# One Trainium2 core: attention, routed experts and a dense layer, with queries in their own order, maxima masked by products, and residues split anew between VectorE and GpSimd

## The chip, the cores and the metric

The kernel runs on one core of a Trainium2 chip. Its time is the device time in microseconds from start to end of one execution; the kernel before took 931.68 us, the median of three runs.

## The reference

Three layers follow each other. Only the first, the attention, is touched by the change.

```python
# q, k, v: (4, 8, 576, 64), s: (4, 8, 576), all float32
scores = scale * np.matmul(q, k.transpose(0, 1, 3, 2))          # scale = 1 / 8
cum = np.cumsum(np.maximum(s, 0.0), axis=-1)
bias = -(cum[:, :, :, None] - cum[:, :, None, :])
scores = np.where(causal, -1e9, scores + np.minimum(bias, 0.0)) # causal: j > i
attn = np.exp(scores - np.max(scores, axis=-1, keepdims=True))
attn = attn / (np.sum(attn, axis=-1, keepdims=True) + 1e-09)
x = np.matmul(attn, v)                                          # -> (2304, 512)
# then: gate = softmax(x @ w_gate), the best of 8 experts for each row:
#   out = gate * (max(x @ w1[e], 0) @ w2[e])                    # 512 -> 1024 -> 512
# then: h = max(out @ w_in, 0); h * h @ w_out                   # 512 -> 2048 -> 512
```

## The kernel before

**Precision.** Each number that goes into a product of the attention is held as two float16 numbers, a high part and a low part (the number less its high part). So every q, k and v is first cast (the high part, lines 428 to 432) and then subtracted (the low part, lines 438 and 441), and the exponentials are split as well: H is the exponential in float16, P the same in float32, and L = P - H the residue.

**Tiling.** The 32 pairs of batch and head (n = 0 to 31) are worked in 8 units u of 4 heads. A unit has tiles kA, qA (both parts of k and q, head dimension on the partitions, made by DMA transposes at line 477 from hlk and hlq) and, three deep in turn, kB and qB (the high part once more, on 64 partitions, with rows for the cumulative bias and for the maxima below them). A head's 576 rows are four blocks of 128 and a tail of 64. In qB the queries stand in another order than in q: `load` fetches them four rows a partition, so the copies into qB (line 501, one a head, and 506, the tails) put them back in order with a strided read; `second_k` (line 559) copies the keys into kB in two pieces.

**Steps of a head.** `maxima` works on pairs of heads: products of the high parts (line 586) into the PSUM tiles mxb and mxt, then on VectorE a maximum over each row's block (line 592: it adds a mask from SBUF while it reads, writes a junk tile, and is followed by an instruction that reads the accumulator out; line 624 is the one maximum that needs no mask). Lines 645 and 646 make high and low parts of the maxima, TensorE transposes them (652), lines 654 or 655 copy them to ms, and a DMA (658) puts them as two rows into qB. Only then can `scores` multiply (lines 679 and 680, with a mask product at 682). `expo` makes P (732) and H (734) on ScalarE, both from the PSUM tile of the scores, and L (736) on GpSimd or VectorE. `pv` multiplies v with H and L (767), and the sums and the division follow (786 to 797). Every few heads the gate of the experts works on finished rows (line 892 and on).

**What sets the order.** `Steps` is a planner: it holds a cost per engine for each step, what the step needs, its buffers and its due time, and lays out one fixed list of instructions per engine. Where a step may go on several engines (`st.add` with several costs) the planner chooses. On the chip each engine works through its list in order, waiting where data are not ready. Gaps that the planner sees on TensorE it fills with products that nobody reads (lines 317 and 324).

After the attention, at about 272 us, the expert and dense loops begin; no line of them is changed.

Of the kernel before, what the change touches and what calls it, by code (L numbers as in the profile page):

```python
# [19 lines left out]
NEG = -1.0e30  # L20
# [154 lines left out]
class Attention:  # L175
# [5 lines left out]


# [7 lines left out]
    LDVE = 6  # L190

    def __init__(self, ctx, tc, keep, q, k, v, s, w_gate, x_dram, tab, base, base0, ident):
# [22 lines left out]
        tags(5, "P")  # L215
        tags(10, "H", "L")
        tags(3, "junk", "ms")
# [46 lines left out]
    def setup(self, moe_constants):  # L264
# [7 lines left out]
        self.mrow, self.mtail = tile("mrow", [128, 512], F32), tile("mtail", [128, 64], F32)  # L272
        self.mT, self.mTt = tile("mT", [128, 128], BF16), tile("mTt", [64, 64], BF16)
        self.tops, self.parts = tile("tops", [128, NP, 9], F32), tile("parts", [128, NP, 18], F16)
# [19 lines left out]
        def mrow():  # L294
            nc.gpsimd.memset(self.mrow, 0.0)
            for i in range(4):
                block(self.mrow[32 * i:32 * i + 32, 384:512], [[-1, 128]], i, 4)

        def mtail():
            nc.gpsimd.memset(self.mtail, 0.0)  # L300
            for i in range(2):
                block(self.mtail[64 * i:64 * i + 64, :], [[-1, 64]], 0, 1)

        def mT():
            nc.gpsimd.memset(self.mT, 0.0)
            block(self.mT.rearrange("j (c p) -> j c p", c=4), [[1, 4], [4, 32]], 0, -1)
# [5 lines left out]
        self.gps("mrow", 1670, mrow)  # L312
# [20 lines left out]
        self.gps("mtail", 700, mtail)  # L333
# [4 lines left out]
    def decay(self):  # L338
# [46 lines left out]
    def load(self, u, w):  # L385
        b, h0 = u // 2, 4 * (u % 2)
        use = [("ld" + w, u)]
        for h in range(0, 4, 2 if w == "q" else 1):
            if w == "q":

                f = lambda eng, h=h: eng.dma_start(
                    out=self.ld(w, u)[:, 4 * h:4 * h + 8, :].rearrange("p (o c) d -> p o (c d)", o=2),
                    in_=self.src[w][b, h0 + h:h0 + h + 2, 0:512, :].rearrange("o (p c) d -> p o (c d)", c=4))
            else:
                f = lambda eng, h=h: eng.dma_start(
                    out=self.ld(w, u)[:, 4 * h:4 * h + 4, :],
                    in_=self.src[w][b, h0 + h, 0:512, :].rearrange("(t p) d -> p t d", p=128))
            self.dma(("ld", w, u, h), f, 730, use=use)
# [13 lines left out]
    def split(self, u, w, eng=None):  # L412
# [31 lines left out]
        for p in pieces:  # L444
            n = 128 if p == "t" else 256 * p[1]
            if p == "t":
                need, use = [("tl", w, b, o) for o in range(2)], [("tl" + w, b), (out, u)]
            else:
                need = [("ld", w, u, h) for h in range(p[0], p[0] + p[1], 2 if w == "q" else 1)]
# [3 lines left out]
            if w != "v" and u < self.LOU:  # L453
                self.st.add(("lo", w, u, p), {"DVE": 1.04 * n + 65, "Pool": 2.1 * n + 90}, lambda e, p=p: lo(p, e),
                            need=[("hi", w, u, p)], use=use)
            else:
                self.dve(("lo", w, u, p), n, lambda p=p: lo(p), need=[("hi", w, u, p)], use=use)
        return pieces

    def turns(self, u):  # L460
# [8 lines left out]
        for i, (b0, nb, gs, what) in enumerate(groups):  # L469
# [11 lines left out]
            need = [("turn", "k", u, i)] + [("eights", "k", u, g) for g in gs if u < 3]  # L481
            if u > 2:
                need.append(("kb", u - 1, 0, "m"))
            for x in what:
                self.dve(("kb", u, i, x), 32 * (nb - nb // 9 if x == "m" and nb > 8 else nb // 9 if nb > 8 else nb),
                         lambda x=x, gs=gs: self.second_k(u, x, gs), need=need, use=[("kA", u), ("kB", u)])
                self.same([("kbx", u, x, g) for g in gs], ("kb", u, i, x))
        gs = (1,) if u == 0 else (0, 1)
        self.dma(("extra", u), lambda eng: self.extra(u, 2 * gs[0], eng), 40, need=["rows"] + (
# [5 lines left out]
        use = [("qA", u), ("qB", u)]  # L495
        for g in range(2):
            pre = [("eights", "q", u, g)] if u < 3 else [("qt", u - 1, 0)]
            for o in range(2):
                h = 2 * g + o
                cs = self.cols(h, 0, 512)  # L500
                self.dve(("qb", u, h), 132, lambda cs=cs: nc.vector.tensor_copy(
                    out=qB[:, cs].rearrange("r (i c p) -> r i c p", c=4, i=4), in_=self.order(A("q")[64:128, cs])),
                    need=pre + [("turned", "q", u, "m", g)], use=use)
        for gs in ((0, 1),) if u else ((0,), (1,)):
            g = slice(gs[0], gs[-1] + 1)
            self.dve(("qt", u, gs[0]), 128 * len(gs) / 4, lambda g=g: nc.vector.tensor_copy(
                out=qB.rearrange("r (g c) -> r g c", g=2)[:, g, 1024:1152],
                in_=A("q")[64:128].rearrange("r (g c) -> r g c", g=2)[:, g, 1024:1152]),
                need=[("turned", "q", u, "t", x) for x in gs] + ([("eights", "q", u, x) for x in gs] if u < 3 else
                                                                 [("qt", u - 1, 0)]), use=use)  # L510
            self.same([("qtail", u, x) for x in gs], ("qt", u, gs[0]))

    def first_turns(self, pieces):
# [3 lines left out]
        for w in "kq":  # L517
            dst = lambda w=w: self.tile(w + "A", 0, [128, 2304], F16)
            for x, b0, nb in ((0, 0, 4), (1, 4, 4), ("t", 8, 1)):
# [18 lines left out]
                if w == "k":  # L538
                    d = slice(512, 576) if x == "t" else slice(576 * x, 576 * x + 512)
                    def second(e, d=d, ps=ps, x=x):  # L540
                        out, src = self.kB[0][0:64, d], ps()[0:64]
                        if x == "t":
                            out = self.kB[0][0:64, 0:1152].rearrange("r (o t) -> r o t", o=2)[:, :, 512:]
                            src = src.rearrange("r (o t) -> r o t", o=2)
                        (nc.scalar.copy if e == "ACT" else nc.vector.tensor_copy)(out=out, in_=src)
# [7 lines left out]
    def second_k(self, u, x, gs):  # L553

        g = slice(gs[0], gs[-1] + 1)
        src = self.tile("kA", u)[0:64].rearrange("r (g c) -> r g c", g=2)[:, g]
        src = (src[:, :, 0:1024] if x == "m" else src[:, :, 1024:]).rearrange("r g (o t) -> r g o t", o=2)
        dst = self.kB[u % 3][0:64].rearrange("r (g o t) -> r g o t", g=2, o=2)[:, g]
        self.nc.vector.tensor_copy(out=dst[:, :, :, 0:512] if x == "m" else dst[:, :, :, 512:], in_=src)

    @staticmethod
    def order(a):
        return a.rearrange("r (c i p) -> r i c p", c=4, i=4)

# [7 lines left out]
    def maxima(self, n):  # L572
# [12 lines left out]
        def mm(out, h, i0, M, j0, N):  # L585
            nc.tensor.matmul(out=out, lhsT=qB[:, self.cols(h, i0, M)], rhs=kB[:, self.S * h + j0:self.S * h + j0 + N],  # L586
                             start=True, stop=True)

        def red(ps, in1, col, init=None):
            w = ps.shape[-1]  # L590
            junk = self.pools["junk"].tile([128, 512], BF16, tag="junk", name=f"junk{n}")
            nc.vector.tensor_tensor_reduce(out=junk[:, 0:w], in0=ps, in1=in1, scale=1.0,  # L592
                                           scalar=2 * NEG if init is None else init,
                                           op0=ALU.add, op1=ALU.max, accum_out=st[:, col:col + 1])
# [5 lines left out]
        def b1r(o, ps):  # L600
            red(ps[:, 0:128], self.mrow[:, 384:512], 4 * o)
            red(ps[:, 128:512], self.mrow[:, 128:512], 4 * o + 2)

# [16 lines left out]
        todo = [("b1", o, 512, lambda ps, o=o: b1(o, ps), 580, lambda ps, o=o: b1r(o, ps)) for o in range(2)]  # L620
        todo += [("b2", o, 512, lambda ps, o=o: mm(ps, h + o, 384, 128, 0, 512), 512,
                  lambda ps, o=o: red(ps, self.mrow, 4 * o + 3)) for o in range(2)]
        todo += [("b3", 0, 512, b3, 580, b3r),
                 ("t1", 0, 520, t1, 512, lambda ps: nc.vector.tensor_reduce(out=st[:, 8:9], in_=ps, axis=AX.X, op=ALU.max)),  # L624
                 ("t2", 0, 66, t2, 126, lambda ps: red(ps[:, 0:64], self.mtail, 8, init=st[:, 8:9]))]
        done = []
        for nm, o, cols, f, el, r in todo:
# [3 lines left out]
            need += [("cum", u, i, g) for i in os] + ([("z", u)] if u > 2 else [])  # L631
# [1108 lines left out]
```

## Time and profile before

| | |
|---|---|
| median of 3 runs | 931.68 us (931.45 to 933.04) |
| the profiled execution, its own time | 932.99 us |
| its span, first to last instruction | 931.5 us |
| mean granted TensorE clock | 0.967 |
| busy over the span: PE, DVE, ACT, POOL | 859.1, 691.9, 479.5, 330.1 us |

A busy share is a mean over stages that differ: the attention (to about 246 us), the handover with the gate's last part (to about 272 us), and the experts and the dense layer. PE, DVE, ACT, POOL and SP are TensorE, VectorE, ScalarE, GpSimd and SyncE.

### The profile page before, as it was taken

The numbers are of one execution on the slowest core, as the hardware profiler recorded it, in microseconds if no ns is written. First come the engines' busy times: TensorE is split into PE (matmuls) and PEld (weight loads), VectorE is DVE, ScalarE is ACT, GpSimd is POOL, SyncE is SP. The second block draws the span as 40 slices with busy tenths as digits, with TensorE's granted clock in tenths as the row PEclk, the third lists the DMA queues.
The fourth block names the chain that finished last, engine by engine and source line by source line (L and its number), as shares of the span: only waits on it lengthen the run. The fifth ranks groups of instructions, "written<-read, shape, count | busy, mean of one in ns | idle before, by whom it ended". The sixth has DMA issues, their size and how long they took to land.

```text
span 931.5 us, 17578 instructions
## 1 busy us (share of the span) xinstructions
PE 859.1 (92%) x6561; PEld 730.5 (78%) x6561; DVE 691.9 (74%) x1404; ACT 479.5 (51%) x1012; POOL 330.1 (35%) x367
## 2 busy tenths in 40 slices
PE   4887977879889999999999999999999999999995
PEld 2566755657689999998999777888888888888894
DVE  8999999998856888899889885554455445444673
ACT  3566766656624454455456444444444445444563
POOL 8858677664642364356333351010001000100100
PEclk9988999888979999999999999999999999999998
DMA  7875885880166766866665300010001000000100
GB/s 150 147 144 114 171 164 146 147 170 3 38 181 221 227 194 191 275 207 213 203 221 174 120 1 1 1 45 1 1 1 46 0 1 11 36 1 0 46 1 24
DMA packets 142780, 94.06 MB, mean 101 GB/s; under 512 B 98484, under 2 KB 127630, under 8 KB 142690
## 3 DMA queue, kind: packets, MB, share of 16 engines
q1 hardware_dynamic: 134385, 78.72, 32.7%
q0 software_dynamic: 4096, 10.19, 3.3%
q10 hardware_dynamic: 4209, 3.97, 1.4%
q8 instruction: 53, 0.87, 0.4%
q14 instruction: 37, 0.30, 0.1%
HBM read 70.16 MB, written 10.02 MB: 86 GB/s over the span
## 4 chain that ended last, share of the span: by engine, by line
PE 58%; issue 6%; DVE 5%; ACT 1%; POOL 0%; POOLq 0%; DVEq 0%; ACTq 0%
PE y_d L1556 7%; PE hd L1476 7%; PE hd L1474 7%; PE hd L1475 7%; PE y_d L1554 6%; PE y_d L1555 6%; PE y_e L1494 3%; PE y_e L1495 3%; PE y_e L1493 3%; PE he L1474 3%; PE he L1475 3%; PE he L1476 3%; DVE wae_6l L1404 1%; DVE wbe_6l L1404 1%; DVE wbe_7l L1404 1%
## 5 line engine op out<-in xcount | busy, mean ns | idle before, releaser
L1599 POOL DMA_INDIRECT out_dram<-o,ids x18 | 18.5, 1027 | 341.9 <-ACT o L1596 339.1
L1542 DVE TENSOR_TENSOR sqd<-hd,rld 128x512 f32<-128x512 f32 (+1 forms) x80 | 50.9, 637 | 112.8 <-ACT rld L1540 111.7
L736 POOL TENSOR_TENSOR L<-P,H 128x512 f16<-128x512 f32 x87 | 104.8, 1218 | 53.6 <-ACT H L734 25.4
L1540 ACT ACTIVATE rld<-hd 128x512 f32<-128x512 f32 (+1 forms) x80 | 44.5, 556 | 130.8 <-PE hd L1476 130.8
L1546 DVE TENSOR_TENSOR ald<-sqd,ahd 128x512 fp32r<-128x512 f32 (+1 forms) x80 | 51.1, 639 | 51.6 <-ACT ahd L1545 51.6
L1545 ACT CAST ahd<-sqd 128x512 fp32r<-128x512 f32 (+1 forms) x80 | 46.3, 579 | 74.2 <-DVE sqd L1542 74.2
L1456 POOL TENSOR_TENSOR lf<-lf,pw 128x512 f32<-128x512 f32 x32 | 50.1, 1566 | 73.4 <-DVE pw L1455 55.1
L732 ACT ACTIVATE P<-tt 128x512 f32<-128x512 f32 x96 | 58.3, 610 | 32.9 <-PE tt L682 14.5
L680 PE MATMUL tt<-qB,kB 128*128 128x128 f16 (+3 forms) x352 | 64.4, 236 | 0.0
L767 PEld LDWEIGHTS <-H 128*128 128x128 f16 x896 | 51.1, 101 | 14.4 <-issue 8.9
L734 ACT ACTIVATE H<-tt 128x512 f16<-128x512 f32 x96 | 58.3, 612 | 6.8 <-PE tt L680 3.8
L1483 ACT ACTIVATE hhe<-he 128x400 fp32r<-128x400 f32 (+7 forms) x64 | 27.9, 436 | 65.1 <-PE he L1476 60.5
L767 PE MATMUL pv<-v,H 128*128 128x65 f16 (+1 forms) x896 | 60.8, 200 | 0.6 <-ACT xb L797 0.3
L679 PE MATMUL tt<-qA,kA 128*128 128x128 f16 (+3 forms) x352 | 59.3, 235 | 1.1 <-ACT H L734 0.9
L592 DVE CUSTOM_DVE_ANT_0 junk<-mxb,mrow 128x128 bf16<-128x128 f32 (+3 forms) x128 | 55.1, 484 | 2.9 <-PE mxb L586 2.6
L767 PE MATMUL pv<-v,L 128*128 128x65 f16 x448 | 55.7, 197 | 1.3 <-DVE L L736 0.8
L1181 POOL DMA_INDIRECT xg<-x_dram,idt x20 | 21.2, 1060 | 85.5 <-PE xps L1191 69.5
L586 PE MATMUL mxb<-kB,qB 128*128 128x128 f16 (+3 forms) x128 | 32.0, 338 | 18.0 <-DVE tops L624 9.5
L767 PEld LDWEIGHTS <-L 128*128 128x128 f16 x448 | 44.1, 103 | 1.5 <-DVE L L736 0.9
L1484 DVE SCALAR_TENSOR_TENSOR hle<-he,hhe 128x400 fp32r<-128x400 f32 (+7 forms) x64 | 30.7, 480 | 17.0 <-ACT hhe L1483 16.8
L679 PEld LDWEIGHTS <-kA 128*128 128x128 f16 (+1 forms) x384 | 35.7, 103 | 6.9 <-issue 2.0
L586 PEld LDWEIGHTS <-qB 128*128 128x128 f16 (+1 forms) x192 | 14.8, 106 | 31.2 <-issue 17.3
(696 smaller groups left out, 3097.4 us busy)
## 6 DMA issues: line engine op xcount, KB each, us to landing
w0s<-in_moe_w_dram SPq DMA_DIRECT2D x30, 512.0 KB
w1s<-in_moe_w_dram SPq DMA_DIRECT2D x30, 512.0 KB
wout<-in_moe_w_in_dram SPq DMA_DIRECT2D x16, 512.0 KB
wout<-in_moe_w_out_dram SPq DMA_DIRECT2D x12, 512.0 KB
ldv<-in_v_dram SPq DMA_DIRECT2D x32, 128.0 KB
ldq<-in_q_dram SPq DMA_DIRECT2D x15, 256.0 KB
ldk<-in_k_dram SPq DMA_DIRECT2D x30, 128.0 KB
x_dram<-xb SPq DMA_DIRECT2D x3, 1024.0 KB
```

Of the source, the lines that this page charges most:

```text
L679: nc.tensor.matmul(out=ps, lhsT=kA[:, j], rhs=a, start=True, stop=False)
L680: nc.tensor.matmul(out=ps, lhsT=kB[:, self.S * h + j0:self.S * h + j0 + M], rhs=qB[:, i], start=False, stop=not mask)
L732: self.act(("P",) + key, w, lambda: nc.scalar.activation(out=P(), in_=ps(), func=AF.Exp, scale=0.125), need=[T], use=[use, ("P", key)])
L734: self.act(("H",) + key, w, lambda: nc.scalar.activation(out=H(), in_=ps(), func=AF.Exp, scale=0.125), need=[T], use=[use, ("H", key)])
L736: f = lambda e="Pool": (nc.gpsimd if e == "Pool" else nc.vector).tensor_tensor(out=L(), in0=P(), in1=H(), op=ALU.subtract)
L767: nc.tensor.matmul(out=ps[0:M, I, 0:N], lhsT=a, rhs=m, start=(i == 0), stop=(i == len(ops) - 1))
L1474: nc.tensor.matmul(out=ps, lhsT=wh[:, k, :], rhs=xh[:, k, 0:C], start=(k == 0), stop=False)
L1475: nc.tensor.matmul(out=ps, lhsT=wh[:, k, :], rhs=xl[:, k, 0:C], start=False, stop=False)
L1476: nc.tensor.matmul(out=ps, lhsT=wl[:, k, :], rhs=xh[:, k, 0:C], start=False, stop=(k == 3))
L1554: nc.tensor.matmul(out=acc[t], lhsT=ah[:, c], rhs=wh, start=first, stop=False)
L1555: nc.tensor.matmul(out=acc[t], lhsT=ah[:, c], rhs=wl, start=False, stop=False)
L1556: nc.tensor.matmul(out=acc[t], lhsT=al[:, c], rhs=wh, start=False, stop=last)
```

## The change

Queries are loaded like keys, one DMA a head, in their own order, so that qB and kB are each one copy of the unit's 2304 columns on VectorE or ScalarE. Maxima get their mask from a product on TensorE (10 more a pair), so that the maximum is a plain reduction. Their high part is now made on ScalarE and their low part on VectorE after the transpose, and two DMAs bring them to qB. H is a copy of P, no longer a second exponential. L may go to VectorE for all heads and not only for the last six, at other prices. Low parts of q and k go to GpSimd alone, the first unit's excepted. P, H and L get more buffers. The bias rows of kB take four DMAs a unit where they took one.

```diff
-    LDVE = 6
+    LDVE = 32
-        tags(5, "P")
-        tags(10, "H", "L")
-        tags(3, "junk", "ms")
+        tags(6, "P")
+        tags(13, "H", "L")
+        tags(3, "ms")
...
-        for h in range(0, 4, 2 if w == "q" else 1):
-            if w == "q":
...
+        for h in range(4):
+            self.dma(("ld", w, u, h), lambda eng, h=h: eng.dma_start(
+                out=self.ld(w, u)[:, 4 * h:4 * h + 4, :],
+                in_=self.src[w][b, h0 + h, 0:512, :].rearrange("(t p) d -> p t d", p=128)), 730, use=use)
...
+            if w != "v" and u > 0:
+                self.gps(("lo", w, u, p), 2.1 * n + 90, lambda p=p: lo(p, "Pool"), need=[("hi", w, u, p)], use=use)
...
+                get = lambda w=w, t=t, r=r, cs=cs: dict(out=t[0:64, cs], in_=A(w)[r, cs])
+                self.st.add((w + "b", u, i), {"DVE": 34 * nb + 65, "ACT": 107 * nb + 55}, lambda e, get=get: (
+                    nc.vector.tensor_copy if e == "DVE" else nc.scalar.copy)(**get()), need=need, use=use)
...
+                nc.tensor.matmul(out=out[:, N - M:], lhsT=self.identb[0:M, 0:M], rhs=self.mQ if M == 128 else self.mQt,
+                                 start=False, stop=True)
...
+        self.dve(("part", n), 5, lambda: nc.vector.tensor_tensor(out=st[:, 8:9], in0=st[:, 8:9], in1=st[:, 9:10], op=ALU.max),
...
+        self.act(("ms", n, 0), 128, lambda: nc.scalar.mul(out=ms()[:, 0, :], in_=ps(), mul=-0.125), need=[("prow", n)], use=use)
+        self.dve(("ms", n), 128, lambda: nc.vector.scalar_tensor_tensor(
+            out=ms()[:, 1, :], in0=ps(), scalar=-0.125, in1=ms()[:, 0, :], op0=ALU.mult, op1=ALU.subtract),
...
-        self.act(("H",) + key, w, lambda: nc.scalar.activation(out=H(), in_=ps(), func=AF.Exp, scale=0.125), need=[T],
-                 use=[use, ("H", key)])
+        self.st.add(("H",) + key, {"ACT": 0.833 * w + 80}, lambda: nc.scalar.copy(out=H(), in_=P()), need=[("P",) + key], use=[("P", key), ("H", key)])
...
-            self.st.add(("L",) + key, {"Pool": 2.09 * w + 45, "DVE": 1.04 * w + 65}, f, **kw)
+            self.st.add(("L",) + key, {"Pool": 2.2 * w + 45, "DVE": 1.4 * w + 100}, f, **kw)
```

**VectorE, third unit.** The lists are in program order, one row an instruction (x2: two alike in a row). Before, where the third unit's keys and queries are copied ahead of the maxima of heads 8 and 9, the names kB2 and qB2 being that unit's tiles:

```order
L559 COPY kB2_124<-kA2_885 64x4x512
L438 SCALAR_TENSOR_TENSOR v1_459<-ldv1_740,v1_459 128x8x64
L789 RECIPROCAL sums_135<-sums_135 128x5
L559 COPY kB2_124<-kA2_885 64x4x64
L794 TENSOR_TENSOR xb0_863<-pv2_897,sums_135 128x5x64
L506 COPY qB2_127<-qA2_976 64x2x128
L501 COPY qB2_127<-qA2_976 64x512 x2
L430 TENSOR_SCALAR v1_459<-ldv1_740 128x8x64
L786 TENSOR_SCALAR sums_135<-pv3_1055 128x5
L501 COPY qB2_127<-qA2_976 64x512
L789 RECIPROCAL sums_135<-sums_135 128x5
L501 COPY qB2_127<-qA2_976 64x512
```

The same place of the changed kernel:

```order
L484 COPY kB2_124<-kA2_1038 64x2304
L700 TENSOR_TENSOR L5_0_1198<-P5_0_1149,H5_0_1185 128x512
L700 TENSOR_TENSOR L5_2_1286<-P5_2_1228,H5_2_1258 128x512
L484 COPY qB2_127<-qA2_1173 64x2304
L750 TENSOR_SCALAR sums_135<-pv4_1181 128x5
L426 TENSOR_SCALAR v1_406<-ldv1_995 128x8x64
L753 RECIPROCAL sums_135<-sums_135 128x5
L434 SCALAR_TENSOR_TENSOR v1_406<-ldv1_995,v1_406 128x8x64
L584 TENSOR_REDUCE tops_134<-mxb1_8_0_1343 128x1 x2
L584 TENSOR_REDUCE tops_134<-mxb1_8_1_1353 128x1 x2
L604 TENSOR_REDUCE tops_134<-mxb3_8_0_1364 128x2
```

Seven copies became two, and two residues L of head 5 have come onto VectorE between them.

**GpSimd, heads 9 to 11.** Before (L10_1 is the second residue of head 10, L10_t that of its tail, hlq4 the fifth unit's queries):

```order
L736 TENSOR_TENSOR L9_2_1900<-P9_2_1787,H9_2_1760 128x512
L736 TENSOR_TENSOR L10_0_1937<-P10_0_1816,H10_0_1799 128x512
L736 TENSOR_TENSOR L10_1_1981<-P10_1_1858,H10_1_1838 128x512
L736 TENSOR_TENSOR L10_2_2028<-P10_2_1876,H10_2_1885 128x512
L441 TENSOR_TENSOR hlq4_1716<-ldq4_1437,hlq4_1716 128x8x64
L441 TENSOR_TENSOR hlq4_1716<-tlq2_1680,hlq4_1716 128x2x64
L736 TENSOR_TENSOR L11_0_2114<-P11_0_1919,H11_0_1941 128x512
```

The same place of the changed kernel:

```order
L700 TENSOR_TENSOR L9_1_1885<-P9_1_1820,H9_1_1842 128x512
L700 TENSOR_TENSOR L10_0_1933<-P10_0_1872,H10_0_1910 128x512
L700 TENSOR_TENSOR L10_1_1978<-P10_1_1929,H10_1_1967 128x512
L437 TENSOR_TENSOR hlk4_1995<-ldk4_1754,hlk4_1995 128x8x64 x2
L437 TENSOR_TENSOR hlq4_2005<-ldq4_1858,hlq4_2005 128x8x64 x2
L437 TENSOR_TENSOR hlk4_1995<-tlk2_1794,hlk4_1995 128x2x64
L437 TENSOR_TENSOR hlq4_2005<-tlq2_1895,hlq4_2005 128x2x64
L700 TENSOR_TENSOR L11_0_2185<-P11_0_2032,H11_0_2045 128x512
```

All low parts of the fifth unit's keys and queries stand here now, and L9_2 and L10_2 have left GpSimd.

**ScalarE, start of head 8.** Before (tt8_0 is the first score tile of head 8, xb0 the output rows):

```order
L732 ACTIVATE P7_2_1503<-tt7_2_1466 128x512
L734 ACTIVATE H7_2_1523<-tt7_2_1466 128x512
L428 ACTIVATE v2_481<-ldv2_1166 128x8x64
L732 ACTIVATE P8_0_1546<-tt8_0_1510 128x512
L797 ACTIVATE xb0_863<-pv5_1335,sums_135 128x64 x5
L734 ACTIVATE H8_0_1578<-tt8_0_1510 128x512
L734 ACTIVATE H8_1_1585<-tt8_1_1537 128x512
L732 ACTIVATE P8_1_1615<-tt8_1_1537 128x512
```

The same place of the changed kernel:

```order
L699 CAST H7_2_1526<-P7_2_1510 128x512
L424 CAST hlq3_1077<-ldq3_1409 128x8x64
L752 ACTIVATE sums_135<-pv6_1462 128x5
L619 ACTIVATE ms8_1566<-mxrow_8_1559 9x128
L424 CAST hlq3_1077<-ldq3_1409 128x8x64
L624 DMA qB2_127<-ms8_1566 1x9x128 x2
L392 DMA ldv2_1484<-in_v_dram 128x4x64
L619 ACTIVATE ms10_1610<-mxrow_10_1605 9x128
L624 DMA qB2_127<-ms10_1610 1x9x128 x2
L484 COPY kB0_122<-kA3_1568 64x2304
L697 ACTIVATE P8_0_1711<-tt8_0_1674 128x512
L697 ACTIVATE P8_1_1713<-tt8_1_1692 128x512
```

The maxima rows of both pairs of the unit (heads 8 and 10) and a copy of the next unit's keys now stand ahead of the first exponential of head 8; before, the rows of head 10 came behind it.

## Rows read from the trace of the kernel before

**Rows 1.** Busy time by stretch: start:end, length, PE, PEld, DVE, ACT, POOL, clock, DMA.

```profile
24.00:246.00 222.00, 182.19 (x2894) 144.49 (x2893) 211.28 (x604) 144.41 (x381) 148.35 (x182) 0.91 0.63 126
272.00:931.00 659.00, 644.52 (x3440) 561.55 (x3440) 440.27 (x687) 315.56 (x589) 148.16 (x129) 0.99 0.28 88
```

**Rows 2.** Waits of DVE, 24 to 246 us: us in total, times, longest.

```profile
DVE junk L592 <- PE mxb L586: 2.6, 6, 0.6
```

**Rows 3.** Waits of all engines, 0 to 246 us.

```profile
POOL L L736 <- ACT H L734: 25.4, 21, 2.9
...
PE mxrow L652 <- DVE parts L646: 14.5, 9, 4.2
```

**Rows 4.** DVE groups, 0 to 275 us: busy us, mean ns, idle before.

```profile
L501 DVE COPY qB<-qA 64x512 f16<-64x512 f16 x32 | 22.1, 718 | 0.3
L441 DVE TENSOR_TENSOR hlk<-ldk,hlk 128x512 f16<-128x512 f32 (+1 forms) x12 | 16.5, 1375 | 0.0
L438 DVE SCALAR_TENSOR_TENSOR v<-ldv,v 128x512 f16<-128x512 f32 (+1 forms) x17 | 16.3, 965 | 0.1
L892 DVE SCALAR_TENSOR_TENSOR xhl<-xb,xhl 128x512 f16<-128x512 f32 x15 | 12.1, 848 | 0.0
...
L624 DVE TENSOR_REDUCE tops<-mxt 128x1 f32<-128x512 f32 x16 | 10.9, 680 | 0.8 <-PE mxt L586 0.8
L559 DVE COPY kB<-kA 64x2048 f16<-64x2048 f16 (+3 forms) x16 | 9.5, 600 | 0.1
L646 DVE SCALAR_TENSOR_TENSOR parts<-tops,parts 128x9 f16<-128x9 f32 x16 | 8.4, 523 | 0.6
L645 DVE TENSOR_SCALAR parts<-tops 128x9 f16<-128x9 f32 x16 | 7.7, 484 | 0.1
L736 DVE TENSOR_TENSOR L<-P,H 128x512 f16<-128x512 f32 x9 | 6.1, 682 | 0.6 <-ACT H L734 0.6
...
L506 DVE COPY qB<-qA 64x256 f16<-64x256 f16 (+1 forms) x9 | 4.9, 549 | 0.2
...
L441 DVE TENSOR_TENSOR hlq<-ldq,hlq 128x512 f16<-128x512 f32 x5 | 3.3, 680 | 0.0
...
L441 DVE TENSOR_TENSOR hlq<-tlq,hlq 128x128 f16<-128x128 f32 x4 | 2.3, 587 | 0.0
...
L654 DVE COPY ms<-mxrow 18x128 f16<-18x128 f16 x8 | 1.7, 208 | 1.1 <-PE mxrow L652 1.0
```

**Rows 5.** DVE groups by shape, 0 to 275 us, the widest copy of keys.

```profile
L559 DVE COPY kB<-kA 64x2048 f16<-64x2048 f16 x7 | 4.8, 693 | 0.0
```

**Rows 6.** Timeline of DVE at three places: start, duration, instruction.

```profile
19.61 0.69 DVE L592 CUSTOM_DVE_ANT_0 junk<-mxb,mrow 128x512 bf16<-128x512 f32 x1
20.22 0.69 DVE L592 CUSTOM_DVE_ANT_0 junk<-mxb,mrow 128x512 bf16<-128x512 f32 x1
...
37.23 0.39 DVE L501 COPY qB<-qA 64x512 f16<-64x512 f16 x1
...
204.34 5.09 DVE L501 COPY qB<-qA 64x512 f16<-64x512 f16 x1
```

**Rows 7.** Timeline of POOL beside the last of these.

```profile
204.53 2.28 POOL L736 TENSOR_TENSOR L<-P,H 128x512 f16<-128x512 f32 x2
...
207.01 2.26 POOL L736 TENSOR_TENSOR L<-P,H 128x512 f16<-128x512 f32 x2
```

**Rows 8.** Groups of ACT by shape, 0 to 275 us: a copy in float16.

```profile
L535 ACT COPY kA<-mxk 128x512 f16<-128x512 f16 x2 | 1.2, 586 | 4.2 <-DVE kB L545 4.2
```

**Rows 9.** Timeline of PE: a row of maxima, and the first scores behind it.

```profile
23.32 0.28 PE L652 MATMUL mxrow<-ident,parts 128*18 128x128 f16 x1 [2.27 <-DVE parts L646]
...
28.20 0.22 PE L679 MATMUL tt<-qA,kA 128*128 128x128 f16 x1
28.25 0.22 PE L680 MATMUL tt<-qB,kB 128*128 128x128 f16 x1
```

**Rows 10.** DMA queues, 0 to 260 us: packets, MB, share of 16 engines.

```profile
q1 hardware_dynamic: 96961, 30.45, 58.7%
```

More of the change, by code (lines that the diff above doesn't have):

```diff
@@ L448, in split @@
             else:
-                need = [("ld", w, u, h) for h in range(p[0], p[0] + p[1], 2 if w == "q" else 1)]
+                need = [("ld", w, u, h) for h in range(p[0], p[0] + p[1])]
                 use = [("ld" + w, u), (out, u)]
@@ L494, in turns @@
                 self.same([("cum", u, o, 0)], ("direct", o))
[L495 to L511, printed above, removed]
+        if u == 0:
+            self.dve(("qb", u, "first"), 32 * 9 + 65, lambda: nc.vector.tensor_copy(
+                out=qB[:, 0:1152], in_=A("q")[64:128, 0:1152]), need=[("eights", "q", u, 0)] + [
+                    ("turned", "q", u, x, 0) for x in "mt"], use=[("qA", u), ("qB", u)])
+            self.same([("qb", u, 0), ("qb", u, 1), ("qtail", u, 0)], ("qb", u, "first"))
     def first_turns(self, pieces):
@@ L538, in first_turns, with second @@
                 if w == "k":
[L539 to L545, printed above, removed]
+                    def second(e, cs=cs, ps=ps):
+                        (nc.scalar.copy if e == "ACT" else nc.vector.tensor_copy)(out=self.kB[0][0:64, cs], in_=ps()[0:64])
                     self.st.add(("kb",) + key, {"ACT": 0.833 * n + 55, "DVE": 0.52 * n + 65}, second,
@@ L585, in mm @@
         def mm(out, h, i0, M, j0, N):
[L586 to L594, printed above, removed]
+            nc.tensor.matmul(out=out, lhsT=qB[:, self.cols(h, i0, M)], rhs=kB[:, self.cols(h, j0, N)],
+                             start=True, stop=j0 + N <= i0)
+            if j0 + N > i0:
+                nc.tensor.matmul(out=out[:, N - M:], lhsT=self.identb[0:M, 0:M], rhs=self.mQ if M == 128 else self.mQt,
+                                 start=False, stop=True)
         def b1(o, ps):
@@ L649, in maxima @@
[L649 to L656 removed]
+            if nm == "b3":
+                f = lambda ps=ps: nc.vector.tensor_reduce(
+                    out=st[:, 1:9].rearrange("p (a b) -> p a b", b=4)[:, :, 0],
+                    in_=ps().rearrange("p (k w) -> p k w", k=2), axis=AX.X, op=ALU.max)
+            else:
+                f = lambda r=r, ps=ps: red(ps(), *r)
@@ new lines, in maxima @@
+            self.dve(("r",) + key, el, f, need=[("m",) + key], use=[mx])
+            done.append(("r",) + key)
+        ps = lambda: self.tile("mx", ("row", n), [128, 512], F32)[0:9, 0:128]
+        ms = lambda: self.tile("ms", n, [9, 2, 128], F16)
+        use = [("mx", ("row", n)), ("ms", n)]
+        self.dve(("part", n), 5, lambda: nc.vector.tensor_tensor(out=st[:, 8:9], in0=st[:, 8:9], in1=st[:, 9:10], op=ALU.max),
+                 need=done)
+        self.pe(("prow", n), 250, lambda: nc.tensor.transpose(ps(), st[:, 0:9], self.ident), need=[("part", n), "moe"], use=use[:1])
@@ L676, in score @@
         j, i = self.cols(h, j0, M), self.cols(h, i0, N)
-        a = qA[:, i] if i0 == 512 else \
-            self.order(qA[:, self.cols(h, 0, 512)])[:, i0 // 128:(i0 + N) // 128]
-        nc.tensor.matmul(out=ps, lhsT=kA[:, j], rhs=a, start=True, stop=False)
-        nc.tensor.matmul(out=ps, lhsT=kB[:, self.S * h + j0:self.S * h + j0 + M], rhs=qB[:, i], start=False, stop=not mask)
+        nc.tensor.matmul(out=ps, lhsT=kA[:, j], rhs=qA[:, i], start=True, stop=False)
+        nc.tensor.matmul(out=ps, lhsT=kB[:, j], rhs=qB[:, i], start=False, stop=not mask)
         if mask:
@@ L844, in ids @@
             B, S = self.B, self.S
[L845 to L848 removed]
+            for a in (0, 2):
+                iota(pr[:, :, :, a], [[S, B], [128, 5]], 0, 1)
         self.dve("wg3", 665, parts, need=["wg"])
```

121 lines of the change are left out of this document (43 added, 78 removed).

## The prediction

> **What bounds the kernel now.** I read the busy time by stretch first [rows 1]. From 272 us on, where experts and dense layer run, TensorE is busy for 644.5 of 659 us; the change touches no line there, so those 659 us are carried over. What can move lies before. From 24 to 246 us VectorE is busy for 211.3 of 222 us, TensorE for 182.2 (products that nobody reads among them), ScalarE for 144.4 and GpSimd for 148.4. A busy share alone proves little, so the waits came next. VectorE's longest sum of waits for one partner in that stretch is 2.6 us in six pieces [rows 2]: it has hardly ever nothing to do. The others wait for work further up: GpSimd 25.4 us for H, and TensorE 14.5 us for the parts of the maxima, which VectorE makes [rows 3]. So VectorE's list sets the length of the attention, and what it is relieved of comes off the time nearly whole, until something else ends last.
>
> VectorE's groups [rows 4] then give the price list, and the timeline [rows 6] says how to use it: a masked maximum recorded at 0.69 us starts at 19.61, and the next one at 20.22, with its accumulator readout between. Records overlap by about 0.08 us, and the readouts lie inside that step. I take 0.08 off every record that I add or remove.
>
> **The change, part by part, on VectorE.** Counts are from the lists of instructions, durations from rows.
>
> (a) Copies to kB and qB. Out go 32, 16 and 9 records of 22.1, 9.5 and 4.9 us [rows 4]: 36.5, less 57 x 0.08, is 31.9 us. In come seven copies of 64x2304 and one of half that (ScalarE takes the others). The nearest row is the key copy of 2048 columns, 0.693 us [rows 5]; times 2304/2048 that is 0.78. A copy in the query loop takes 0.39 us when nothing disturbs it [rows 6] and 0.718 on average [rows 4]; I add half of that excess of 0.33, since fewer, longer copies meet GpSimd less often, and get 0.95, or 0.87 a step. Seven and a half of them make 6.5. Net -25.4 (between -26.6 with clean copies and -24 with the whole excess).
>
> (b) Low parts of q and k. 12 + 5 + 4 records of 16.5, 3.3 and 2.3 us go to GpSimd [rows 4]; the four smallest ones that rows 4 leave out stand for the four that remain on VectorE. 22.1 less 21 x 0.08 is -20.4.
>
> (c) Maxima. A plain reduction of 512 columns takes 0.680 us [rows 4], the masked one 0.69 [rows 6]: nothing is gained by width. Two of 256 columns become one of 512, which saves one start a pair: -1 for 16 pairs.
>
> (d) Parts of the maxima. Lines 645 and 646 go: 16.1 us less 32 x 0.08 is 13.5 [rows 4]. In come 16 maxima of one column, which I price like line 645 at 0.484 (0.40 a step, 6.5 us; the end below is 0.1 each), and 16 low parts in place of 8 copies to ms at 0.208 (0.13 a step, +1.0). Net -6.0.
>
> (e) Residues L. VectorE gets 38 wide ones in place of 9: 29 more. Its nine now average 0.682 us [rows 4], which gives 0.60 a step and 17.5 us in all; but these stand in the last six heads. Elsewhere VectorE's other 128x512 instructions with operands in SBUF are longer: the four rows of lines 441, 438 and 892 (12, 5, 17 and 15 instructions, 16.5, 3.3, 16.3 and 12.1 us) average 48.2/49 = 0.98. I take that, 0.90 a step: +26.2. The upper end is line 441 on keys, 1.375: 37.6. Six more tails at some 0.4 add 2.4.
>
> High casts and norms move by a few in either direction and are taken at nothing.
>
> The sum is -25.4 - 20.4 - 1 - 6.0 + 26.2 + 2.4 = **-24**, between -33 and -13 by the ends of (e) alone.
>
> **What is laid on others, and what hides it.** TensorE gets 160 mask products. Two products of 128 columns follow each other by 0.05 us [rows 9], so that is 8 us, against 40 us idle in the stretch and the fillers besides. ScalarE gets seven copies of 64x2304 and two halves: by 0.586 us for 512 columns [rows 8] 2.6 us each, 21 us in all, against 78 us idle. If its cover is gone at one place, it delays one P by 2.6 us. H no longer needs the score bank, which comes free one exponential earlier, but must wait for P; there is room for that in the 78 us too. GpSimd loses 29 wide residues at 1.14 us [rows 7] and gets 15 wide low parts of a like size and seven narrow ones: it comes out some 12 us less busy. SyncE issues one DMA more a pair for the maxima, 15 more for q and three more a unit for the bias; its queue isn't what VectorE waits for.
>
> **What is given back.** In the third and the sixth unit the first scores now stand behind the maxima of both pairs: the rows of head 10 precede the first exponential of head 8 in ScalarE's list, where they came later before. From the transposed row of a pair to the first scores behind it 4.9 us pass (23.32 to 28.20 [rows 9]), and the row has one more DMA and one more hop to VectorE now. VectorE has the residues of the heads before to work on meanwhile, but these end. I take 4 us for each of the two places, 8 in all (ends: 0, where the residues last, and 10). With that the change is worth **-16 us**.
>
> The sum is made on the profiled execution of 932.99 us, 931.5 of them its span and 1.5 around it; it gives 917. That execution lies 1.3 us above the median of the three runs, so against 931.68 the same sum gives **915.5**.
>
> **A rule weighed.** A query copy that takes 0.39 us undisturbed took 5.09 at 204.34 [rows 6], while GpSimd worked from 204.53 through two residues, a tail and two more, to 209.27 [rows 7]: it ended with the last of these. The Trainium skill ("SBUF — State Buffer", section "Who interferes with whom") says that a VectorE instruction with two SBUF inputs, or a copy in a two-port mode, and a GpSimd instruction that reads SBUF exclude each other: whichever issues first holds the shared ports for its whole instruction and the other blocks. By that rule a residue on VectorE would take at most one GpSimd residue more, 0.60 + 1.14 = 1.74 us; were half of that wait met every time, (e) would be +34 and the forecast 923. The trace agrees that the two engines block each other, but not on the limit: the copy waited through five instructions, not one. This speaks against residues on both engines at once, and the rival on the other side rests on it.
>
> **The rivals.**
>
> 1. *Cleaner.* Low parts, copies and single-column parts leave VectorE, so it meets GpSimd less often, and its residues stay at 0.60 a step; (e) is 17.5, and the drains are covered. Then -33: 899, or up to 905 with a part of it. For it: the nine residues that are there already. Against: those overlap with a GpSimd that has few other things to do.
>
> 2. *The chain of the maxima takes it back.* All pairs, not two units, wait for their longer way from maximum to row; half of 4.9 us in each of the eight units, 20 us in place of 8, leaves -4: about 927. For it: TensorE waits 14.5 us for these parts already [rows 3]. Against: the maxima of most units stand a unit ahead of their scores.
>
> 3. *Other side: GpSimd locks VectorE out of its residues.* Where GpSimd has several instructions ready, VectorE's one waits for all of them, as at 204.34. If 5 of the 29 residues cost 5.09 and the others 0.98, (e) grows by 5 x 4.1 = 20.5 and the time is 936. It decides once the 29 average 0.98 + 16/29 = 1.53 us, over line 441's 1.375, now the worst row of its kind. For it: residues of one head stand on both engines now, and get their inputs at the same time. Against: GpSimd's own load falls.
>
> 4. *DMA.* The 16 query loads go from pieces of 1 KB to 256 B: 4096 packets become 16384. The queue's 96961 packets take 58.7% of 16 engines over 260 us [rows 10], 25 ns each; 12288 more are 310 us, 19.4 us on each of 16 engines. Wholly on the path that gives 935; hidden it is nothing. The engines are busy for 63% of the stretch [rows 1], and loads run a unit ahead, so I expect nothing of it but for the first unit. The Trainium skill ("DMA: Bandwidth & Descriptors", section "Specifications") asks for at least 512 B a transfer for the line rate and so speaks for this rival; by the packets of this trace, 314 B on average, most of the traffic is below that size already.
>
> **How the numbers follow.** The forecast (905 to 924) gets 0.55; the first rival 0.13, below 905. The second gets 0.16: 0.11 of it faster, 924 to 929.8, and 0.05 within 0.2% of before, which is 1.9 us and about what a measurement of this kernel can tell from no change. The other side gets 0.16, 0.12 for GpSimd's lock and 0.04 for the DMA. So faster 0.79, same 0.05, slower 0.16. The range reaches from 899, the sum with every end of (e) on the good side, to 934, where the two rivals on the other side begin to bite.
>
> **What would show it.** In the changed profile: VectorE's busy time between 24 us and the end of the attention lower by 20 to 30 us, with the attention itself ending near 230 us; eight copies to kB and qB on VectorE at 0.8 to 1.1 us; 38 wide residues at 0.9 to 1.1; the single-column maxima near 0.4; VectorE's waits grown from few to about 8 us, most of them ahead of heads 8 and 20 for H; the stretch from the attention's end to the last instruction as long as before. Wrong it would be if residues on VectorE average over 1.5 us, if VectorE waits 15 us or more for products of the maxima or for H, or if the first maxima start later than now because q comes late.

## The result, and the profile after

The changed kernel takes 921.91 us (median of four runs, 920.81 to 923.68), the kernel before beside it 932.36. The ratio is 0.9885, with a 95% interval of 0.9859 to 0.9912. The profiled execution took 920.81 us, its span 919.3.

The busy time up to the last division of the attention, at 246 us before and 242 after, and from the first expert products on (columns as in [rows 1]). Before:

```profile
0.00:246.00 246.00, 193.94 (x2959) 151.38 (x2960) 232.76 (x661) 153.20 (x399) 167.88 (x220) 0.92 0.64 129
```

After:

```profile
0.00:242.00 242.00, 206.73 (x3284) 167.60 (x3285) 203.15 (x471) 174.67 (x406) 157.62 (x205) 0.99 0.66 134
260.00:919.00 659.00, 644.85 (x3440) 561.99 (x3440) 440.77 (x687) 316.12 (x591) 147.41 (x129) 0.99 0.27 88
```

VectorE is busy for 203.2 us in place of 232.8: 29.6 us less. The 659 us of experts and dense layer are the same as before. TensorE's granted clock up to the last division (third number from the right) was 0.92 before and is 0.99 after. But VectorE waits now (its waits, 24 to 246 us, for [rows 2]):

```profile
DVE tops L584 <- PE mxb L562: 10.2, 5, 4.9
DVE ms L620 <- ACT ms L619: 3.9, 5, 1.2
DVE tops L604 <- PE mxb L562: 3.8, 1, 3.8
...
DVE tops L584 <- PE mxt L559: 2.4, 2, 2.2
...
DVE tops L584 <- PE mxt L562: 1.6, 4, 0.7
```

The four rows of L584 and L604 are waits for products of the maxima, 18.0 us together. 8.0 of them lie at one place, while TensorE has the scores of heads 20 and 21 ahead of these products:

```profile
168.75 1.42 DVE L584 TENSOR_REDUCE tops<-mxb 128x1 f32<-128x128 f32 x4 [4.22 <-PE mxb L562]
...
173.98 0.69 DVE L604 TENSOR_REDUCE tops<-mxb 128x2 f32<-128x512 f32 x1 [3.81 <-PE mxb L562]
```

The first maximum of all starts 2.75 us later. Before and after:

```profile
16.94 0.69 DVE L624 TENSOR_REDUCE tops<-mxt 128x1 f32<-128x512 f32 x1
```

```profile
19.69 0.75 DVE L584 TENSOR_REDUCE tops<-mxb 128x1 f32<-128x128 f32 x2 [0.91 <-PE mxb L562]
```

Its groups, 0 to 275 us, for [rows 4]:

```profile
L700 DVE TENSOR_TENSOR L<-P,H 128x512 f16<-128x512 f32 x38 | 30.5, 810 | 2.1 <-ACT H L699 2.0
L584 DVE TENSOR_REDUCE tops<-mxb 128x1 f32<-128x512 f32 x32 | 21.0, 677 | 0.3 <-PE mxb L562 0.3
...
L616 DVE TENSOR_TENSOR tops<-tops 128x1 f32<-128x1 f32 x16 | 6.5, 405 | 0.0
...
L620 DVE SCALAR_TENSOR_TENSOR ms<-mxrow,ms 9x128 f16<-9x128 f32 x16 | 4.4, 273 | 4.0 <-ACT ms L619 3.9
L484 DVE COPY qB<-qA 64x2304 f16<-64x2304 f16 x4 | 3.7, 931 | 2.3 <-DMA qA<-hlq 2.2
...
L484 DVE COPY kB<-kA 64x2304 f16<-64x2304 f16 x3 | 3.3, 1114 | 0.0
```

Where the 12.2 us of span came from is read at two marks, the last division and the first expert product, from the timelines of VectorE and TensorE before,

```profile
245.72 0.49 DVE L794 TENSOR_TENSOR xb<-pv,sums 128x320 f32<-128x320 f32 x1
...
272.33 0.66 PE L1474 MATMUL he<-xhf,ahw 128*128 128x400 f32 x1 [2.62 <-DVE wae_1l L1404]
```

and of ScalarE and TensorE after:

```profile
240.83 1.13 ACT L761 ACTIVATE xb<-pv,sums 128x64 f32<-128x64 f32 x5 [0.43 <-DVE sums L753]
...
260.26 0.42 PE L1436 MATMUL he<-xhf,ahw 128*128 128x400 f32 x1 [1.60 <-DVEq L1468]
```

The last division ends at 246.21 and 241.96: the attention is 4.2 us shorter. From there to the first expert product it was 26.1 us and is 18.3: **the handover is 7.8 us shorter**, and nearly two thirds of the gain lie there. The granted clock in it is much the same, 0.80 and 0.81. In it the rows of the leading expert are gathered on GpSimd. The first gather before and after:

```profile
247.50 1.18 POOL L1181 DMA_INDIRECT xbg<-x_dram,idtf  x1 [5.11 <-DMA idtf<-tab]
```

```profile
231.63 1.54 POOL L1143 DMA_INDIRECT xbg<-x_dram,idtf  x1 [1.53 <-PE tt L645]
```

It stands behind the gate of the third batch, whose last step on VectorE (slots) ends the list of places. Before and after:

```profile
222.83 0.25 DVE L962 TENSOR_REDUCE g_lg<-olg 128x40 f32<-128x120 f32 x1
...
233.60 0.17 DVE L983 CAST slots<-g_slot 128x5 int32<-128x5 f32 x1
```

```profile
212.22 0.28 DVE L924 TENSOR_REDUCE g_lg<-olg 128x40 f32<-128x120 f32 x1 [0.27 <-PE olg L893]
...
219.30 0.16 DVE L945 CAST slots<-g_slot 128x5 int32<-128x5 f32 x1
```

That gate begins 10.6 us earlier and passes VectorE in 7.1 us in place of 10.8, so the gather now runs beside the last heads, where it stood behind the last division.

### The profile page after: what moved, and what is told of

The parts are those of the page before. It is cut to its first block, busy times and chain, and to the rows that moved or that the text cites. A ratio compares the mean times of both kernels' runs of the same rounds, so it can differ in the third digit from the quotient of the medians.

```text
span 919.3 us, 17959 instructions
## 1 busy us (share of the span) xinstructions
PE 866.9 (94%) x6865; PEld 742.5 (81%) x6865; DVE 657.2 (71%) x1205; ACT 498.1 (54%) x1011; POOL 315.7 (34%) x348
## 4 chain that ended last, share of the span: by engine, by line
PE 59%; issue 6%; DVE 5%; ACT 1%; POOL 0%; POOLq 0%; DVEq 0%; ACTq 0%
PE y_d L1518 7%; PE hd L1438 7%; PE hd L1437 7%; PE hd L1436 7%; PE y_d L1516 7%; PE y_d L1517 6%; PE y_e L1456 3%; PE y_e L1457 3%; PE y_e L1455 3%; PE he L1436 3%; PE he L1438 3%; PE he L1437 3%; DVE wae_6l L1366 1%; DVE wbe_6l L1366 1%; DVE wbe_7l L1366 1%
## 5 line engine op out<-in xcount | busy, mean ns | idle before, releaser
L1502 ACT ACTIVATE rld<-hd 128x512 f32<-128x512 f32 (+1 forms) x80 | 44.4, 555 | 130.6 <-PE hd L1438 130.6
L700 POOL TENSOR_TENSOR L<-P,H 128x512 f16<-128x512 f32 x58 | 72.3, 1255 | 42.9 <-ACT H L699 31.5
L697 ACT ACTIVATE P<-tt 128x512 f32<-128x512 f32 x96 | 54.9, 594 | 17.4 <-PE tt L647 7.3
L645 PE MATMUL tt<-qB,kB 128*128 128x128 f16 (+3 forms) x352 | 58.4, 225 | 5.2 <-DMA qB<-ms 5.2
L644 PE MATMUL tt<-qA,kA 128*128 128x128 f16 (+3 forms) x352 | 54.8, 226 | 4.5 <-ACT P L697 4.5
L731 PE MATMUL pv<-v,H 128*128 128x65 f16 (+1 forms) x896 | 55.5, 194 | 3.5 <-ACT xb L761 3.2
L699 ACT CAST H<-P 128x512 f16<-128x512 f32 x96 | 56.9, 617 | 1.4 <-DVE ms L620 1.2
L731 PEld LDWEIGHTS <-H 128*128 128x128 f16 x896 | 46.7, 96 | 7.9 <-issue 3.8
L731 PE MATMUL pv<-v,L 128*128 128x65 f16 x448 | 51.4, 191 | 0.4 <-POOL L L700 0.4
L584 DVE TENSOR_REDUCE tops<-mxb 128x1 f32<-128x128 f32 (+2 forms) x96 | 43.8, 500 | 11.1 <-PE mxb L562 11.1
L645 PEld LDWEIGHTS <-kB 128*128 128x128 f16 (+1 forms) x384 | 33.0, 99 | 11.9 <-DMA qB<-ms 5.7
```

The source lines that it names most:

```text
L644: nc.tensor.matmul(out=ps, lhsT=kA[:, j], rhs=qA[:, i], start=True, stop=False)
L645: nc.tensor.matmul(out=ps, lhsT=kB[:, j], rhs=qB[:, i], start=False, stop=not mask)
L697: self.act(("P",) + key, w, lambda: nc.scalar.activation(out=P(), in_=ps(), func=AF.Exp, scale=0.125), need=[T], use=[use, ("P", key), ("H ...
L699: self.st.add(("H",) + key, {"ACT": 0.833 * w + 80}, lambda: nc.scalar.copy(out=H(), in_=P()), need=[("P",) + key], use=[("P", key), ("H", ...
L700: f = lambda e="Pool": (nc.gpsimd if e == "Pool" else nc.vector).tensor_tensor(out=L(), in0=P(), in1=H(), op=ALU.subtract)
L731: nc.tensor.matmul(out=ps[0:M, I, 0:N], lhsT=a, rhs=m, start=(i == 0), stop=(i == len(ops) - 1))
```

## The experiments

Each kernel was timed in five rounds beside the kernel before on the same chip, and ratios are to that. Chips differ (the kernel before took 933 to 940 us), so ratios are compared, not times. From the first expert product to the end all fourteen profiles take 658 to 659 us, so the differences lie ahead of it. The slowest chip ran e1 to e4, and no trace of the changed kernel was taken there: their marks in us are compared with each other.

**Undoing a part.** e1 lets low parts go to either engine again, e2 takes the residues of all but the last six heads off VectorE, e3 leaves the copies to VectorE alone.

```diff
 e1
-            if w != "v" and u > 0:
+            if w != "v" and u >= self.LOU:
 e2
-    LDVE = 32
+    LDVE = 6
-            self.st.add(("L",) + key, {"Pool": 2.2 * w + 45, "DVE": 1.4 * w + 100}, f, **kw)
+            self.st.add(("L",) + key, {"Pool": 2.09 * w + 45, "DVE": 1.04 * w + 65}, f, **kw)
 e3
-                self.st.add((w + "b", u, i), {"DVE": 34 * nb + 65, "ACT": 107 * nb + 55}, ...
+                self.st.add((w + "b", u, i), {"DVE": 34 * nb + 65}, ...
```

> The changed kernel, but low parts of q and k may go to VectorE or GpSimd as before (19 of them come back to VectorE where the changed kernel has 4; it gives up 6 residues and 4 whole-unit copies for them). VectorE's own work grows by about 15 x 0.95 - 6 x 0.73 - 4 x 0.87 + 4 x 0.4 = 8 us. Theory A (VectorE now idles some 29 us before the last division, because chains through ScalarE and TensorE hold the attention up): most of it goes into the idle time, 919 to 925 us. Theory B (VectorE's work still sets the end): the whole 8 us, about 930 us.

> The changed kernel, but residues L on VectorE for the last six heads alone, at the old prices (13 there in place of 46; GpSimd gets 33 more, some 40 us). Theory A (GpSimd's list is what the split relieves; alone it would hold up the products with v): 926 to 935 us, with TensorE waiting for L on GpSimd. Theory B (VectorE's work sets the end, and its residues are locked out by GpSimd): VectorE is relieved of 24 us less some 5 for norms and copies that come to it, so 905 to 915 us.

> The changed kernel, but all 16 whole-unit copies to kB and qB on VectorE (7 now; nine of 2.1 us or half that leave ScalarE's list). Theory A (a copy that stands in ScalarE's list waits there for its DMA transpose and holds up P and H of the heads in work): the waits of GpSimd for H fall, and the attention is 3 to 6 us shorter, 915 to 919 us. Theory B (VectorE's work sets the end): nine copies more at 0.87 less 7 residues fewer at 0.73, +3 us, about 925 us.

e1: 0.9949 (0.9917 to 0.9980), which on the 931.7 us of before is 927 us: between the two theories, 2 us above A's range. VectorE's busy time up to the last division is 205.3 us, only 2 more than in the changed kernel where 8 were expected, so e1 doesn't decide between them. e2: 1.0105 (1.0050 to 1.0161), slower than before and further off than A expected. Its last division comes at 270.4 us. Up to there:

```profile
0.00:270.40 270.40, 221.02 (x3284) 178.15 (x3284) 195.29 (x440) 166.19 (x376) 186.41 (x238) 0.93 0.61 120
```

VectorE is busy for 195.3 us, 8 less than in the changed kernel, in the slowest kernel of all: its busy time doesn't set the end there. The wait that A named is small (TensorE's weight loads waited 4.3 us for L on GpSimd), so what holds e2 up is not shown by one row. e3: 0.9900 (0.9847 to 0.9953), an interval that reaches from the one theory's range to the other's and can't be told from the changed kernel. GpSimd's wait for H is no shorter (37.6 us against 31.5, on another chip), so nothing speaks for copies in ScalarE's list as its cause.

**The handover.** e4 asks for the third batch's gate later.

```diff
-    GD2 = 0.5
+    GD2 = 5
```

> The changed kernel, but the due time of the third batch's gate is moved back (GD2 from 0.5 to 5 head times), so that it and the choice of the leading expert stand late in VectorE's list, as they did before the change. Theory A (the stretch from the last division to the first expert product, 18.3 us now and 26.1 before, is short because the leading expert's rows are gathered and multiplied beside the last heads): that stretch goes back to 24 to 27 us, and the time to 926 to 930 us. Theory B (it is short for another reason, such as a less busy GpSimd): no change, 921 us.

0.9972 (0.9943 to 1.0001): 8 us of the gain are gone. The gather has moved behind the last division (241.2 us), and the first expert product begins at 276.2 us, 35.0 us after it, even later than theory A said; e1, e2 and e3, on the same chip, have 22.3, 20.2 and 21.3 us there. VectorE and GpSimd:

```profile
242.27 0.76 DVE L945 CAST slots<-g_slot 128x5 int32<-128x5 f32 x1
```

```profile
254.47 0.98 POOL L1143 DMA_INDIRECT xbg<-x_dram,idtf  x1 [4.39 <-DMA idtf<-tab]
```

Theory A holds: when the leading expert is known sets the handover. The other profiles say the same. The handover takes 18.3 to 18.8 us where the first gather begins 10 to 11 us ahead of the last division (the changed kernel, e5, e6), 20.2 to 21.3 where it begins 7 to 8 ahead (e2, e3, e8), 22.3 and 23.0 at 2.3 and 2.4 ahead (e1, e9), and 25.1 to 26.1 at 1 to 3 behind (before, e7, e10, e12). Only e11 stands apart, with 21.6 at 10.8 ahead; its granted clock there is 0.68. The 8 us of e4 are not the worth of the early gate alone: the gate stands later than in the kernel before (242.3 against 233.6), and the attention ends earlier than in e1 and e3 (249.1 and 251.1).

**Taking work away.** e5 is the changed kernel again; e6 and e7 shorten the wide maxima in the changed kernel and in the one before, so that the columns of older keys are left out; e9 and e10 are the same with the planner told. In e6:

```diff
-        ... ((0, 128, 4 * o, 1), (128, 384, 4 * o + 2, 1))
+        ... ((0, 128, 4 * o, 1), (384, 128, 4 * o + 2, 1))
-        ... ((0, 512, 4 * o + 3, 1),)
+        ... ((384, 128, 4 * o + 3, 1),)
-        ... ("t1", 0, 520, t1, 520, ((0, 512, 8, 1),))
+        ... ("t1", 0, 520, t1, 520, ((384, 128, 8, 1),))
...
-                    in_=ps().rearrange("p (k w) -> p k w", k=2), axis=AX.X, op=ALU.max)
+                    in_=ps().rearrange("p (k w) -> p k w", k=2)[:, :, 128:256], axis=AX.X, op=ALU.max)
```

> The changed kernel as it is, for comparison on the chip of the next three: every theory expects its earlier ratio to the kernel before, 0.986 to 0.991.

> The changed kernel, but the wide maxima read only the last 128 columns of their block (the keys of the diagonal block; the older keys are left out of the maximum, which the softmax, being unchanged by a shift, tolerates with these inputs); products, order and all else stay. VectorE loses some 32 us of work (32 x 0.27 + 32 x 0.40 + 16 x 0.27 + 16 x 0.40). Theory A (VectorE no longer sets the end, its waits do): 3 to 14 us off, ratio to before 0.974 to 0.986. Theory B (VectorE's work still sets the end): 25 to 32 us off, ratio 0.954 to 0.962.

> The kernel before with the same cut of the maxima, its masks cut alike; order as before. VectorE loses the same 32 us. Theory A of the prediction (VectorE's list sets the length of the attention before): 22 to 30 us off, ratio 0.968 to 0.976, clearly more than the same cut gives the changed kernel. Rival (VectorE was not the bound before either, though it hardly waited): 5 to 14 us off, ratio 0.985 to 0.995.

> As e6 (maxima of the changed kernel read the last 128 columns alone, the older keys left out of them), but the planner is told the shorter costs and lays out new lists. Theory C (the fixed lists, laid out for the longer work, hold the attention up, so work taken from one engine turns into waits): with new lists 8 to 20 us come off, ratio 0.967 to 0.980. Theory D (another engine or chain than VectorE's work sets the end whatever the order): no change against the changed kernel, ratio 0.986 to 0.991.

> As e7 (the same cut of the maxima in the kernel before), with the planner told the shorter costs. Theory C: 10 to 25 us more than the 7 us of e7, ratio 0.966 to 0.982. Theory D: as e7, ratio 0.990 to 0.994.

| | ratio | interval |
|---|---|---|
| e5, changed | 0.9881 | 0.9865 to 0.9897 |
| e6, changed, narrow maxima | 0.9904 | 0.9884 to 0.9923 |
| e9, the same, planned for | 0.9942 | 0.9920 to 0.9964 |
| e7, before, narrow maxima | 0.9920 | 0.9899 to 0.9942 |
| e10, the same, planned for | 0.9936 | 0.9911 to 0.9961 |

Up to the last division, e6 and e7:

```profile
0.00:245.60 245.60, 210.39 (x3283) 170.49 (x3284) 174.43 (x471) 175.06 (x405) 157.76 (x205) 0.97 0.65 132
```

```profile
0.00:240.00 240.00, 192.10 (x2961) 149.39 (x2961) 207.41 (x662) 152.93 (x400) 168.05 (x220) 0.93 0.65 132
```

In the changed kernel VectorE loses another 28.7 us (203.2 to 174.4) and the time doesn't fall at all. In the kernel before it loses 25.4 (232.8 to 207.4), and the last division comes 6 us earlier, the median 7.5 us (0.8%). So before the change too, only a quarter of what VectorE is relieved of, or a little more, came off the time: neither theory's range for e6, the rival's for e7. Most of the rest came back as waits for the products of the maxima: 0 to 246 us, all such rows together grew from 18.9 to 44.4 us in the changed kernel and from 4.6 to 17.7 in the one before. The largest row of each (e6, then e7, where [rows 2] had 2.6):

```profile
DVE tops L584 <- PE mxb L562: 21.2, 26, 5.1
```

```profile
DVE junk L592 <- PE mxb L586: 12.3, 22, 1.3
```

New lists laid out for the shorter maxima don't help (e9, e10): theory C falls. D holds for e10; e9 came out above D's range too. e9 is slower than e6 through the handover: its gather begins at 242.5 us and its first expert product 23.0 us after the last division.

**Other suspects.** e8 brings the bias rows with one DMA a unit, e11 leaves out most products with residues, e12 is the kernel before with q in 256 B pieces.

```diff
 e8
...
-            for c, r in ((to[:, 0:1024], rows[:, :, 0:512]), (to[:, 1024:], rows[:, :, 512:])):
-                eng.dma_start(out=c.rearrange("a (h t) -> a h t", h=2), in_=r)
+        eng.dma_start(out=self.kB[u % 3][64:67, 1152 * g0:2304].rearrange("a (g t) -> a g t", t=1152),
+                      in_=self.rows[2 * u + g0:2 * u + 2].rearrange("g a t -> a g t"))
 e11
-                ops += [(hi, v[:, 0:65], 65, M), (hi, v[:, 65:129], 64, M), (lo, v[:, 0:65], 65, M)]
+                ops += [(hi, v[:, 0:65], 65, M), (hi, v[:, 65:129], 64, M)] + [(lo, v[:, 0:65], 65, M)] * (J == min(I, 3))
 e12
...
+                    for i in range(2):
+                        eng.dma_start(out=self.ld(w, u)[:, 4 * (h + i):4 * (h + i) + 4, :],
+                                      in_=self.src[w][b, h0 + h + i, 0:512, :].rearrange("(t p) d -> p t d", p=128))
```

> The changed kernel, but the bias rows lie in DRAM in the order of kB's columns, so that one DMA a unit brings them where the changed kernel has four (24 fewer issues, 0.65 to 0.8 us each on SyncE's queue; three more issues at the start). Theory A (SyncE's queue delays loads and transposes, and through them the maxima that VectorE waits for): 2 to 6 us off, ratio 0.982 to 0.987. Theory B (that queue is waited for by nobody): no change, ratio 0.9885.

> The changed kernel, but of the products of v with the residues only the last one of each row of blocks is made (160 of 448; the others are left out, so most of the residues' share of the output is missing); lists otherwise the same, and all residues are still made. TensorE loses 288 products of 65 columns, at about 0.03 us each some 9 us in the attention. If TensorE's work set the end: 7 to 9 us off, ratio 0.978 to 0.982. If the waits between the engines do (theory C): 0 to 3 us off, ratio 0.985 to 0.989.

> The kernel before, but q comes in 32 loads of 256 B pieces as in the changed kernel, where it has 16 of 1 KB pieces (the queries stand in another order than the copies take them to be, so the rows are mixed up; the work is the same). The prediction's account (hidden but for the first unit): within 3 us of before, ratio 0.997 to 1.003. Its fourth rival (the DMA time of the smaller pieces on the path): up to 19 us slower, ratio 1.01 to 1.02.

e8: 0.9915 (0.9895 to 0.9934), no gain: theory A falls. Its profile says more. VectorE's waits for products of the maxima fell from 18.0 to 10.4 us, and the gap beside heads 20 and 21 is closed (0.60 us in place of 4.22 and 3.81), but the last division comes at 241.7 us, 242.7 in e5 on the same chip. So that gap didn't set the end by itself, or the residues took back what closing it gave: e8's 39 wide ones on VectorE average 1.009 us, not 0.810. e11: 0.9923 (0.9899 to 0.9948), no gain either and above both ranges, though TensorE has 288 products fewer; TensorE's work alone doesn't set the end. e12: 0.9981 (0.9966 to 0.9997): the small pieces cost nothing. The DMA queue, 0 to 260 us, for [rows 10]:

```profile
q1 hardware_dynamic: 108721, 30.45, 60.4%
```

11760 packets more, but the share went from 58.7 to 60.4%: 1.7% of 16 x 260 us is 71 us, 6 ns for each packet added, not 25 (one execution each).

No variant beat the changed kernel.

## Why the prediction was right, and where it was not

The direction and the range were right; the forecast of 915.5 was 6.4 us low. Term by term:

- **VectorE's work.** Forecast -24, measured -29.6 busy up to the last division (overlaps and a few instructions of the gate included). The copies came near their price (0.93 and 1.11 us against 0.95), so did the plain maxima (0.677) and, a little cheaper, the single-column ones (0.405 against 0.484). Low parts of ms were dearer (0.273 against 0.208). By each line's busy time up to the last division, with no overlap taken off, the terms are (a) -29.0, (b) -21.3, (c) -2.8, (d) -6.9 and (e) +28.8, so none is far off. In (e) two errors met: the wide residues were cheaper (0.810 us on average, a little nearer to the clean 0.682 than to 0.98), the tails, at 0.723 and not some 0.4, dearer.
- **"Comes off the time nearly whole" is the step that failed.** I read it from 211 busy us of 222 and 2.6 us of waits. e7 shows that in that same kernel 25 us less work on VectorE shorten the attention by 6, and e6 shows a kernel with a far emptier VectorE that is no faster. An engine can be busy nearly all the time and wait for almost nothing, and the stretch can still end only a few microseconds earlier when a large part of its work is taken away.
- **"What is given back".** I took 8 us for two drains. Of 29.6 us the attention kept 4.2: 25 us were given back, near the 20 of the second rival. In the sixth unit the drain came, as 8.0 us of waits for products of the maxima and not for H, where I took 4; e8 closes it without a gain, so it isn't a separate cost that adds up. Nor did taking out copies from ScalarE's list (e3), products (e11) or maxima (e6) give anything back. Two of my signs of being wrong came: the waits for products of the maxima are 18.0 us, over the 15 that I named, and the first maximum starts 2.75 us later; TensorE begins the transposes of the first unit's wide query tiles at 13.45 us, before at 6.46.
- **"The stretch behind the attention as long as before"** failed as well, the other way: 7.8 us shorter, since the third batch's gate passes VectorE's list sooner. I looked for VectorE's relief only where its list ends, not at the chain gate, leader, gather that hangs on one place inside it. The attention came out 12 us longer than forecast and the handover 8 us shorter; that the forecast came near is luck, owed to the two errors' opposite signs. With the handover as long as before, this attention would have given some 928 to 930 us, which is the second rival's range and not the forecast's.
- **The rivals.** GpSimd's lock (the third) did not come: the residues average 0.810 us, far from the 1.53 at which it would have decided. By the rule of the Trainium skill, "SBUF — State Buffer", section "Who interferes with whom", half of a GpSimd residue's wait each time would have made them 1.17 us; these 38 have a median of 0.682 and a longest of 1.646, so most met no wait. That depends on the order of the lists: e8's 39 average 1.009. The fourth rival is refuted by e12, where pieces under the 512 B of the Trainium skill ("DMA: Bandwidth & Descriptors", section "Specifications") cost no time.

What stays open is which chain sets the attention's length. Followed back from the last division, in the way in which part 4 of the page goes back from the last instruction, the chain of the kernel before lies for 139 of 245 us on VectorE and 48 on TensorE; in e7 it is 114 and 99; in e5, the changed kernel, 73 and 109, and 31 on DMAs, 16.5 of those the rows of maxima on their way to qB. So the chain went over to TensorE's list with what its instructions wait for. That is a reading of one execution each (of the changed kernel's first profile the chain can be followed only to 133 us), and no experiment took that chain apart: e11 took work off TensorE alone and gained nothing. Trimming the rows' way (maxima, transpose, two hops, two DMAs) was not tried.

A rival for the attention's 4.2 us stands untested, TensorE's granted clock. It rose from 0.92 to 0.99 in this stretch, and the same 352 products of the scores (line 680, now 645) took 58.4 us in place of 64.4. The twelve runs of e1 show clock and time going together: 0.984 in the shortest, 929.1 us, and 0.974 in the longest, 938.9. Whether the shorter attention comes from VectorE's relief or from the clock, and which of clock and waits leads the other, no run separates. The handover is not touched by this, as its clock is the same in both.

## What to carry to other kernels

Before summing what an engine is relieved of, test the premise: cut a large piece of its work, whatever that does to the values, and see how much comes off. Where a planner keeps five in-order lists dense, 25 us of relief on the busiest engine can be worth 6. And look for single steps in the relieved list on which a later stage hangs: here the shorter handover (7.8 us) was worth more than the shorter attention (4.2). Last, compare the granted clock of the two traces before a small difference is put down to the work that was moved.

## What was not expected of the hardware

Four times the packets from the same bytes of q cost 6 ns of DMA time each where the queue's mean is 25 ns, and no time (0.9981). Beside 66 wide and narrow residues on GpSimd, VectorE's 38 wide ones still average 0.810 us, when its copy in the kernel before was once held for 5.09 us [rows 6]; in e8, with another order, 39 average 1.009.
